# Sinkhorn-sorted attention feeding a gated MLP: the last batch's spatial products in two token parts, output tiles in load buffers, and a new hand-written order

## The chip, the cores and the metric

The kernel runs on one core of a Trainium2 chip. A core has five engines that run their own instruction streams and wait for each other by semaphores: TensorE (PE; its weight loads are shown as PEld), VectorE (DVE), ScalarE (ACT), GpSimd (POOL) and SyncE (SP). Sixteen DMA engines move data between HBM and the on-chip memory; here POOL issues the loads, which also cast f32 to bf16, and SP issues copies on the chip, transposes and the stores. The metric is the device time of one execution in microseconds; the time before is 164.44 us, the median of 3 runs (163.99 to 164.55).

## The reference

Two modules in a row, for 4 batches, 768 tokens, 8 heads of 64. The sequence is cut into 8 blocks of 96 tokens. A Sinkhorn-normalised 8x8 matrix for each batch and head mixes the blocks of K and V, attention runs inside each block, and a gated MLP with a spatial (token by token) product follows.

```python
P = sort_net
for _ in range(5):
    P = P - np.max(P, axis=-1, keepdims=True)
    P = np.exp(P)
    P = P / (np.sum(P, axis=-1, keepdims=True) + 1e-09)
    P = P / (np.sum(P, axis=-2, keepdims=True) + 1e-09)
k_sorted = np.einsum('bhij,bhjcd->bhicd', P, k_b)      # blocks of k mixed
v_sorted = np.einsum('bhij,bhjcd->bhicd', P, v_b)
scores = scale * np.matmul(q_b, k_sb.transpose(0, 1, 2, 4, 3))
attn = softmax(scores)
x = concat_heads(np.matmul(attn, v_sb))                # (4, 768, 512)
h = np.maximum(x @ w_in, 0.0)                          # d_ff = 1024
u, v = h[..., :512], h[..., 512:]
v_n = (v - mean(v)) / np.sqrt(var(v) + 1e-06)
v_s = np.einsum('ts,bsd->btd', w_spatial, v_n) + b_spatial[None, :, None]
out = (u * v_s) @ w_out
```

## The kernel before

The whole program is a list of short units, written out by hand in the string `ORDER` (from line 18) and issued in that order; no scheduler moves anything. Each engine gets its own part of every unit, in the order of the list, so a unit's place sets its place in each engine's queue. PSUM is four tiles, ps0 to ps3; most units name the tile that they use, and a unit must wait until the tile's last reader is done. A letter A, D or P in a unit names the engine that copies its result or multiplies: ACT, DVE or POOL.

The units, with the lines of their main instructions in the profile:

- `S0`, `SK` (L231 to L244): the Sinkhorn rounds, on ACT and DVE alone. `MC` (L210) and `MA` (L204) spread the identity and make a mask; `MB` (L207) casts the mask. `DM` (L219): matmuls on zeros that keep PE busy at the start.
- `PR` (L249) replicates the normalised matrices with PE; `P0` (L263, DVE) and `PC` then `PD` (L275, POOL) make the mixing matrices `pd`.
- `L` issues a load on POOL. Load tiles come from one pool of 8 buffers, `ld`. Loads are numbered onto 8 semaphore lanes, so a load's issue also waits for the landing of the load eight before it.
- `QT`, `QQ` (L307): q transposed. `KT` (L363): K mixed and transposed in one matmul, then copied to one of `NK` = 5 tiles `kt`; with two letters (AD, DA) the copy is made in two halves, one on each engine. `VT`, `VB` (L363, L381): the same for V of batch 0; `VM` (L390) and `VC` (L403, eight copies by SP for a batch) for V of the others.
- `SC` (L422, then the exponential on ACT, L427): scores of two heads and four blocks. `AT` (L468; L475 and L476 on DVE): attention times V, divided by the sums. `XT` (L498) or, for batches 2 and 3, `XD` (L486, a DMA transpose): the result turned for the MLP.
- `VP` (L514; relu on L113 ACT or L115 DVE): the v half of x @ w_in. `ST`, `LN`, `LA` (L531, L537, L543): its statistics and normalisation. `UP` (L557): the u half. `WT` (L504): the spatial weights turned.
- `SP` (L569): one spatial product, 128 features by all 768 tokens, 12 matmuls of 384 columns; DVE adds the bias (L575) into a tile `z` (two buffers). `GT` (L585): u times z into `gt`, on DVE or POOL. `BI` (L188) loads the bias.
- `OP` (L595): the output product for two tiles of 128 tokens, 16 matmuls of 512 columns (or fewer, when it is given a range of the four feature chunks); `OE` (L107 ACT or L109 DVE) copies it out of PSUM into a tile `o_sb`, two buffers; `OS` (L610) stores it.
- `CK` (L618 to L622), `CF` (L634 to L636), `LF` (L639): checks that the sums of the fast path stay in range, reduces them to a flag, and loads the flag into a register on every engine. At the end of the program a branch on that register goes to a general path, which is not taken here.

Where the order stands around the change: the last stage begins with `VP` of batch 3; its four `SP`, `GT` and the output products end the list, with `CK` and the last `OP` parts mixed, and `CF:2 LF` as the last two units.

Of the kernel before, what the change touches and what calls it, by code (L numbers as in the profile page):

```python
# [23 lines left out]
AT:0:0:1:1 SC:2:0:1:0 SC:3:0:2:1 AT:1:0:3:1 VM:2:A:1:0 AT:0:0:1:0 VM:3:A:1:1 AT:1:0:2:1 VM:2:A:1:2 XT:0:D:0:1:0
KT:3:A:1:2 AT:1:0:2:0 KT:0:A:1:0 AT:2:0:3:0 XT:3:A:0:1:2 KT:0:A:1:3 QQ:1:D:1:0 VM:2:A:1:3 XT:0:D:0:0:2 XT:3:D:0:0:0
SC:1:1:0:0 QQ:2:D:1:2 VC:1:0:4 KT:0:A:1:1 VP:1:D:0:0:1 SC:3:1:2:1 ST:0:0 SC:0:1:3:1 VP:2:A:0:4:5 WT:3:A:5 WT:1:D:4
VP:0:A:0:3 ST:0:5 PD:2:0:4 SC:2:1:1:0 ST:0:3 SC:1:1:2:0 UP:3:A:0:1:0 VP:2:A:0:2 VC:1:4:8 ST:0:1 ST:0:4 AT:0:1:0:0
ST:0:2 WT:1:A:3 SC:3:1:3:0 LN:0:0:6 UP:2:A:0:0:1 AT:0:1:2:0 AT:1:1:3:0 LA:0:0 PD:2:4:8 UP:3:A:0:1:1 WT:0:D:0 LA:0:2
# [5 lines left out]
OE:A:0:2 L:k:3:0:8 AT:1:2:3:1 VM:2:A:3:2 UP:3:A:1:1:0 ST:1:5 AT:0:2:2:1 ST:1:3 VM:2:D:3:1 L:q:3:0:8 UP:1:A:1:0:1
AT:3:2:1:1 LN:1:0:6 UP:0:A:1:1:1 LA:1:1 AT:1:2:3:0 OP:2:0:0 LA:1:0 SC:1:2:0:1 SC:0:2:2:0 OP:3:0:4 LA:1:5 OS:0:2
OE:D:0:0 LA:1:3 LA:1:4 LA:1:2 AT:2:2:0:1 AT:0:2:2:0 SP:1:1:0 OE:A:0:4 XD:2:1 SC:2:2:0:0 KT:0:DA:3:2 QQ:3:D:3:2
KT:1:D:3:1 KT:2:AD:3:0 SP:0:1:2 KT:2:A:3:3 OS:0:4 GT:D:1:0 QQ:1:A:3:0 AT:3:2:1:0 AT:0:2:0:0 VP:2:D:2:4:5 VC:3:0:4
VC:3:4:8 SC:3:3:3:0 SC:1:3:3:1 ST:2:4 XD:2:0 SP:0:1:1 SC:2:3:2:1 GT:D:1:2 SC:1:3:1:1 SP:3:1:3 AT:0:3:3:0 GT:P:1:3
AT:2:3:3:1 VP:1:A:2:2:3 ST:2:5 VP:0:A:2:0:1 OS:0:0 AT:1:3:2:1 GT:P:1:1 ST:2:3 UP:2:D:2:0:1 OP:1:1:2 SC:3:3:0:0
OE:D:1:2 ST:2:2 SC:2:3:1:0 UP:0:A:2:1:0 SC:1:3:0:1 ST:2:1 ST:2:0 LN:2:0:6 SC:3:3:2:0 UP:2:D:2:0:0 AT:0:3:1:1 LA:2:5  # L40
LA:2:4 LA:2:2 OS:1:2 UP:1:A:2:1:1 OP:2:1:0 AT:1:3:0:0 OE:A:1:0 LA:2:0 LA:2:3 LA:2:1 OP:3:1:4 AT:2:3:1:0 AT:0:3:2:0
SP:1:2:1 XD:3:0 AT:2:3:0:1 XD:3:1 GT:D:2:1 OE:A:1:4 SP:0:2:0 SP:1:2:3 GT:D:2:0 SP:0:2:2 OS:1:4 UP:3:D:3:0:0 OS:1:0
VP:0:D:3:2:3 GT:D:2:2 VP:1:A:3:0:1 ST:3:3 GT:D:2:3 ST:3:2 UP:3:A:3:0:1 VP:0:A:3:4:5 ST:3:1 OP:3:2:2 ST:3:0 OP:2:2:0
# [19 lines left out]
def kernel(  # L63
# [538 lines left out]
    def u_OE(eng, b, n0, lo=0, hi=2):  # L602
        b, n0, lo, hi = int(b), int(n0), int(lo), int(hi)
        if ("o", b, n0) not in st:
            st["o", b, n0] = moe.tile([128, 2, DM], FP32, name="o_sb", tag="o", bufs=2)
        copy(eng, st["o", b, n0][:, lo:hi], st["o_ps", b, n0][:, lo:hi])

    def u_OS(b, n0, lo=0, hi=2):
# [4 lines left out]
        )  # L613

    def u_CK():
        nc.vector.memset(bad, 0.0)  # L618
# [109 lines left out]
```

## Time and profile before

| | us |
|---|---|
| median of 3 runs | 164.44 |
| the profiled execution, its own time | 163.99 |
| its span in the profile | 162.2 |
| PE busy | 147.9 (91%) |
| DVE busy | 117.7 (73%) |
| ACT busy | 84.3 (52%) |
| POOL busy | 33.7 (21%) |

| line | engine, operation | count | mean ns |
|---|---|---|---|
| L569 | PE, spatial product, 384 columns | 192 | 326 |
| L595 | PE, output product, 512 columns | 93 shown of 96 | 379 |
| L575 | DVE, z = product + bias, 768 columns | 16 | 957 |
| L585 | DVE, u times z, 768 columns | 9 | 948 |
| L585 | POOL, u times z, 768 columns | 7 | 1640 |
| L107 / L109 | ACT / DVE, copy of 1024 output columns | 7 / 2 | 1012 / 1219 |
| L107 / L109 | ACT / DVE, copy of 512 output columns | 5 / 1 | 588 / 692 |
| L107 / L109 | ACT / DVE, whole K copy, 768 columns | 7 / 2 | 800 / 952 |
| L107 / L109 | ACT / DVE, half K copy, 384 columns | 7 / 7 | 482 / 549 |
| L476 | DVE, attention result divided | 32 | 687 |
| L543 | DVE, normalisation of 512 columns | 24 | 402 |

Mean times of matmuls contain the depth of the pipeline; in a run of many, a matmul of 512 columns follows the one before after about 0.213 us. A busy PE is therefore not PE at its peak, and the idle time before an instruction says what it waited for.

### The profile page before, as it was taken

How to read it: one execution, taken by the hardware profiler on the slowest of the kernel's cores; microseconds unless marked ns; L12 is line 12 of the kernel's file. 1: busy time of each engine (PE TensorE's matmuls, PEld its weight loads, DVE VectorE, ACT ScalarE, POOL GpSimd, SP SyncE). 2: the span in 40 equal slices, each digit the busy share in tenths (PEclk: the TensorE clock that was granted, in tenths of full speed). 3: DMA queues.
4: the chain of work that ended last, by engine and by line, in shares of the span. 5: the costliest groups of instructions: out<-in, count | busy, mean ns of one | idle time of the engine just before them, and what ended most of it. 6: DMA issues, size and time to landing. Idle time of an engine off the chain costs nothing.

```text
span 162.2 us, 3967 instructions
## 1 busy us (share of the span) xinstructions
PE 147.9 (91%) x1646; PEld 89.5 (55%) x1657; DVE 117.7 (73%) x265; ACT 84.3 (52%) x118; POOL 33.7 (21%) x39
## 2 busy tenths in 40 slices
...
GB/s 12 191 204 205 203 205 205 210 220 237 271 206 204 206 172 0 69 133 148 184 188 94 225 149 195 0 36 97 0 107 237 113 0 0 91 172 129 129 250 25
DMA packets 27351, 23.20 MB, mean 143 GB/s; under 512 B 7232, under 2 KB 24128, under 8 KB 27328
## 3 DMA queue, kind: packets, MB, share of 16 engines
...
q14 instruction: 9, 0.07, 0.1%
HBM read 24.78 MB, written 6.29 MB: 192 GB/s over the span
## 4 chain that ended last, share of the span: by engine, by line
PE 78%; ACT 7%; DVE 6%; DMA 2%; issue 2%; DVEq 0%; ACTq 0%
PE ps L569 20%; PE ps L557 13%; PE ps L514 13%; PE ps L595 11%; PE ps L468 4%; PE ps L422 4%; PE ps L363 3%; PE ps L390 3%; PE ps L307 3%; ACT ex L427 2%; ACT kt L107 2%; PE ps L498 2%; DMA out_dram<-o_sb 1%; PE ps L504 1%; ACT o_sb L107 1%
## 5 line engine op out<-in xcount | busy, mean ns | idle before, releaser
L569 PE MATMUL ps<-wspT,v_sb 128*128 128x384 bf16 x192 | 33.2, 326 | 0.0
L427 ACT ACTIVATE ex<-ps 96x768 bf16<-96x768 f32 x32 | 24.4, 806 | 12.4 <-PE ps L422 12.3
L585 POOL TENSOR_TENSOR gt<-z,u_sb 128x768 bf16<-128x768 f32 x7 | 11.4, 1640 | 92.7 <-DVE z L575 42.1
L569 PEld LDWEIGHTS <-v_sb 128*128 128x128 bf16 x192 | 18.2, 98 | 11.9 <-issue 0.2
L575 DVE TENSOR_TENSOR z<-ps,b_bc 128x768 f32<-128x768 f32 x16 | 15.3, 957 | 11.6 <-PE ps L569 11.5
L557 PE MATMUL ps<-xT,w_in_sb 128*128 128x384 bf16 x128 | 23.3, 326 | 0.0
L476 DVE TENSOR_TENSOR x_sb<-ps,rec_all 96x512 bf16<-96x512 f32 x32 | 22.0, 687 | 1.1
L514 PE MATMUL ps<-w_in_sb,xT 128*128 128x512 bf16 x89 | 22.2, 379 | 0.4
L595 PE MATMUL ps<-w_out_sb,gt 128*128 128x512 bf16 x93 | 22.0, 379 | 0.2
L107 ACT COPY o_sb<-ps 128x1024 f32<-128x1024 f32 (+1 forms) x12 | 9.8, 835 | 14.8 <-PE ps L595 12.9
L531 DVE BATCH_NORM_STATS2 stats<-v_sb 128x6 f32<-128x512 bf16 x24 | 16.2, 677 | 1.0 <-ACT v_sb L113 0.9
L113 ACT ACTIVATE v_sb<-ps 128x1024 bf16<-128x1024 f32 (+1 forms) x8 | 7.4, 920 | 17.6 <-PE ps L514 17.6
L557 PEld LDWEIGHTS <-w_in_sb 128*128 128x128 bf16 x128 | 11.8, 98 | 7.6
L595 PEld LDWEIGHTS <-gt 128*128 128x128 bf16 x96 | 9.2, 98 | 10.2
L514 PEld LDWEIGHTS <-xT 128*128 128x128 bf16 x96 | 9.0, 98 | 9.6 <-DVE x_sb L476 0.2
L113 ACT ACTIVATE u_sb<-ps 128x768 bf16<-128x768 f32 x13 | 10.6, 812 | 5.1 <-PE ps L557 5.0
L107 ACT CAST kt<-ps 128x768 bf16<-128x768 f32 (+1 forms) x14 | 8.7, 641 | 7.9 <-PE ps L363 5.5
L468 PEld LDWEIGHTS <-ex 96*128 96x128 bf16 x256 | 10.5, 97 | 3.6 <-issue 0.3
L468 PE MATMUL ps<-vb,ex 96*128 96x65 bf16 x256 | 11.9, 193 | 0.1
L219 PE MATMUL ps<-warm 128*128 128x512 bf16 x35 | 9.9, 436 | 1.3 <-DVE warm L192 1.3
L422 PE MATMUL ps<-qT,kt 64*128 64x96 bf16 x256 | 9.5, 204 | 1.6 <-ACT kt L107 1.3
L422 PEld LDWEIGHTS <-kt 64*128 64x128 bf16 x256 | 6.2, 94 | 6.9 <-issue 3.8
...
## 6 DMA issues: line engine op xcount, KB each, us to landing
...
```

Source lines behind the costliest of these rows:

```text
L107: nc.scalar.copy(out=out, in_=in_)
L113: nc.scalar.activation(out=out, in_=in_, func=AF.Relu)
L422: nc.tensor.matmul(t[:, hh, 0:HW].rearrange("p (g x) -> p g x", g=G)[:, :, ii * TB:(ii + 1) * TB], lhsT=kT[rows, i * BLK:i * BLK + 128], r ...
L427: nc.scalar.activation(out=e_tile(b, hp, ih).rearrange("p h (x g) -> p h x g", g=G), in_=t[0:BLK, :, 0:HW].rearrange("p h (g x) -> p h x g ...
L468: nc.tensor.matmul(t[:, hh, ii * VW:ii * VW + D + 1], lhsT=e[:, c:c + 128], rhs=vb[b % 2][:, ih * NI + ii, 2 * hp + hh, 0:D + 1], start=Tr ...
L476: nc.vector.tensor_mul(out=x_sb[:, hp].rearrange("p i (h d) -> p h i d", h=2), in0=tv[:, :, :, 0:D], in1=_raw_ap(rec, 0, [rec.ap[0], [NI, ...
L514: nc.tensor.matmul(t[:, x, :], lhsT=st["xT", b][:, n // 3, kc, (n % 3) * 128:(n % 3 + 1) * 128], rhs=w_in_sb[:, kc, DH:DFF], start=(kc == ...
L531: nc.vector.bn_stats(out=stats, in_=st["v_sb", b, n])
L557: nc.tensor.matmul(t[:, x, 0:HW], lhsT=w_in_sb[:, kc, mc * 128:(mc + 1) * 128], rhs=st["xT", b][:, ih, kc, :], start=(kc == 0), stop=(kc = ...
L569: nc.tensor.matmul(t[:, x, 0:HW], lhsT=st["v_sb", b, n][:, mc * 128:(mc + 1) * 128], rhs=wspT[:, 3 * x:3 * x + 3, n, :], start=(n == 0), s ...
L575: nc.vector.tensor_add(out=z.rearrange("p (x c) -> p x c", x=2), in0=t[:, :, 0:HW], in1=b_bc.rearrange("p (x c) -> p x c", x=2),)
L595: nc.tensor.matmul(t[:, x, :], lhsT=st["gt", b, mc][:, (n0 + x) * 128:(n0 + x + 1) * 128], rhs=w_out_sb[:, mc, :], start=(mc == 0), stop=( ...
```

## The change

The helpers gain two sizes, and the output tiles move to the load pool:

```diff
-    NE = 5
+    NE, NK, NZ, NX = 5, 6, 3, 4
...
-    NK = 5
...
-            st["x", b, ih] = att.tile([BLK, HP, NI, 128], BF16, name="x_sb", tag="x", bufs=3)
+            st["x", b, ih] = att.tile([BLK, HP, NI, 128], BF16, name="x_sb", tag="x", bufs=NX)
...
-        z = moe.tile([128, S], FP32, name="z", tag="z", bufs=2)
+        z = moe.tile([128, S], FP32, name="z", tag="z", bufs=NZ)
...
-            st["o", b, n0] = moe.tile([128, 2, DM], FP32, name="o_sb", tag="o", bufs=2)
+            st["o", b, n0] = ld.tile([128, 3, DM], FP32, name="o_sb", tag="ld")[:, 0:2]
```

New units for the last batch: `SH` is a spatial product for tokens 0 to 511 (part 0) or 512 to 767 (part 1), with its own bias sum; `GH` multiplies one part by u; `OH`, `OI` and `OJ` make, copy and store the output of one token tile for a range of columns. (Two more new units, `WW` and `XX`, are not in the order.)

```diff
+    def u_SH(ps, b, mc, c):
+        t, x = ps_tile(ps)[:, 0], tokens(c)
+        w = x.stop - x.start
+        for n in range(G):
+            nc.tensor.matmul(
+                t[:, 0:w], lhsT=st["v_sb", b, n][:, mc * 128:(mc + 1) * 128],
+                rhs=wspT[:, x.start // 128:x.stop // 128, n, :],
+                start=(n == 0), stop=(n == G - 1),
+            )
+        st["z", b, mc, c] = z = moe.tile([128, S], FP32, name="z", tag="z", bufs=NZ)[:, 0:w]
+        nc.vector.tensor_add(out=z, in0=t[:, 0:w], in1=b_bc[:, x])
+    def u_GH(eng, b, mc, c):
...
+        eng.tensor_mul(out=st["gt", b, mc][:, x], in0=st["z", b, mc, c], in1=st["u", b, mc // 2][:, mc % 2, x])
+    def u_OH(ps, b, n, c0, c1, lo=0, hi=4):
...
+        for mc in range(lo, hi):
+            nc.tensor.matmul(
+                st["o1_ps", b, n, c0], lhsT=st["gt", b, mc][:, n * 128:(n + 1) * 128], rhs=w_out_sb[:, mc, c0:c1],
...
+    def u_OI(eng, b, n, c0, c1):
+        st["o1", b, n, c0] = ld.tile([128, 3, DM], FP32, name="o1_sb", tag="ld")[:, 0, 0:c1 - c0]
+        copy(eng, st["o1", b, n, c0], st["o1_ps", b, n, c0])
+    def u_OJ(b, n, c0, c1):
+        nc.sync.dma_start(out=out[b, n * 128:(n + 1) * 128, c0:c1], in_=st["o1", b, n, c0])
```

The order is written anew from end to end. Its beginning, the part where batch 2's K begins, and its end:

```diff
-S0 CO SK:0 L:q:0:0:8 L:k:0:0:8 L:v:0:0:8 L:v:1:0:8 BH SK:1 SK:2 L:k:1:0:8 ID IV:2 MC IV:0 DM:1:6:512 L:q:1:0:8 SK:3
-L:wv MA DM:3:6:512 DM:1:6:512 DM:2:6:512 SK:4 L:wsb QT:1:A:0:0 MB QT:0:D:0:1 QT:3:A:0:2 DM:2:6:512 PR:3 DM:2:6:512
-P0:0:2 KT:1:A:0:0 P0:6:8 L:wu P0:4:6 PC:D P0:2:4 PD:1:0:4 QT:0:D:0:3 L:wsa IV:1 PD:1:4:8 KT:2:DA:0:1 KT:3:DA:0:3
+S0 CO L:q:0:0:8 SK:0 L:k:0:0:8 ID SK:1 DM:1:6:512 DM:2:6:512 SK:2 MC L:v:0:0:8 DM:0:6:512 MA L:v:1:0:8 IV:0 L:k:1:0:8
+SK:3 L:q:1:0:8 DM:1:6:512 DM:3:6:512 DM:2:6:512 SK:4 QT:1:A:0:0 PR:2 MB QT:0:A:0:3 P0:6:8 P0:4:6 L:wv L:wu L:wsa
+P0:2:4 P0:0:2 QT:3:D:0:1 PC:A KT:1:A:0:1 KT:0:A:0:0 BH PD:1:4:8 L:wsb QT:3:D:0:2 IV:2 KT:2:D:0:2 SC:1:0:1:1 L:v:2:0:8
+SC:0:0:0:0 PD:1:0:4 KT:3:D:0:3 SC:2:0:1:0 L:k:2:0:8 VT:1:D:0:1 SC:0:0:2:0 SC:3:0:0:1 VT:2:D:0:0 VB:0:D:0:1 VT:1:A:0:2
...
-GT:P:0:3 KT:1:AD:2:3 KT:3:AD:2:2 KT:0:DA:2:0 KT:2:A:2:1 GT:P:0:2 QQ:1:A:2:0 SC:0:2:3:0 VM:3:D:2:3 SP:2:0:1 VM:1:A:2:2
+SP:1:0:1 SP:2:0:2 SC:0:1:2:0 AT:1:1:0:0 KT:3:A:2:3 GT:P:0:2 XT:2:A:1:1:2 KT:0:D:2:1 KT:3:A:2:0 QQ:1:D:2:0 GT:P:0:1
+QQ:2:D:2:2 KT:0:A:2:2 AT:3:1:2:0 SP:1:0:0 SC:3:2:0:0 XT:0:D:1:1:0 XT:2:A:1:0:0 XT:1:D:1:0:2 AT:3:2:0:0 SC:0:2:1:0
...
-SP:3:3:0 GT:P:3:2 SP:0:3:1 OP:2:2:4 GT:D:3:1 OS:2:0 OS:2:2 OE:A:2:4 GT:D:3:0 SP:3:3:3 OP:1:3:0:0:3 GT:D:3:3
-OP:0:3:4:0:3 OP:-1:3:0:3:4 OE:A:3:0:1:2 OP:3:3:2:0:3 CK OS:2:4 OP:-1:3:2:3:4 OE:D:3:2:1:2 OE:A:3:0:0:1 OP:-1:3:4:3:4
-OS:3:0:1:2 OS:3:0:0:1 OE:A:3:2:0:1 OS:3:2:0:1 OS:3:2:1:2 OE:A:3:4:0:1 OS:3:4:0:1 OE:A:3:4:1:2 OS:3:4:1:2 CF:2 LF
+CK OE:D:1:0 SP:3:2:3 GT:P:2:3 CF:0 SP:2:2:2 VP:0:A:3:0:1 VP:1:D:3:2:3 VP:3:A:3:4:5 ST:3:2 ST:3:5 OS:0:4 SP:2:2:0
+ST:3:1 SP:3:2:1 GT:P:2:0 UP:0:A:3:0:1 GT:D:2:2 ST:3:3 UP:2:A:3:0:0 UP:3:A:3:1:0 ST:3:4 ST:3:0 LN:3:0:6 LF LA:3:0
+GT:P:2:1 OP:2:2:0 OS:1:2 OE:D:2:0 LA:3:2 OP:0:2:4 LA:3:3 LA:3:5 OP:3:2:2 OE:A:2:2 LA:3:4 LA:3:1 OS:1:0:0:1 OS:1:0:1:2
+SH:2:3:0:0 GH:P:3:0:0 OS:2:2:0:1 OS:2:2:1:2 SH:1:3:1:0 OS:1:4 OE:A:2:4 GH:D:3:1:0 SH:0:3:2:0 UP:1:D:3:1:1 GH:D:3:2:0
+OS:2:0:0:1 OS:2:0:1:2 SH:2:3:3:0 SH:3:3:0:1 SH:1:3:1:1 GH:P:3:3:0 OS:0:0 GH:D:3:0:1 OS:2:4:0:1 OS:2:4:1:2 SH:0:3:3:1
+SH:2:3:2:1 OP:3:3:0 GH:P:3:1:1 OE:D:3:0 GH:P:3:2:1 OP:2:3:2 GH:P:3:3:1 OH:3:3:5:0:256:0:4 OI:D:3:5:0:256 OE:A:3:2
+OS:3:0 OH:1:3:4:0:512:0:4 OJ:3:5:0:256 OI:D:3:4:0:512 OS:3:2 OH:2:3:5:256:512:0:4 OI:A:3:5:256:512 OJ:3:4:0:512
+OJ:3:5:256:512
```

In it every K copy is whole (11 on ACT, 5 on DVE); of the products u times z, 10 whole ones and 5 parts are POOL's, 2 whole ones and 3 parts DVE's; `CK`, `CF` and `LF` stand before or within the last batch's MLP; and `BI` stands between the two `VC` of batch 1.

More of the change, by code (lines that the diff above doesn't have):

```diff
@@ L24 @@
[L24 to L28, printed above, removed]
@@ L34 @@
[L34 to L38, printed above, removed]
@@ L39 @@
[L39 to L43, printed above, removed]
@@ L44 @@
-ST:3:5 ST:3:4 OE:A:2:2 LN:3:0:6 UP:1:A:3:1:1 LA:3:1 UP:0:A:3:1:0 LA:3:5 LA:3:3 LA:3:0 LA:3:2 OE:A:2:0 LA:3:4 SP:1:3:2
-SP:3:3:0 GT:P:3:2 SP:0:3:1 OP:2:2:4 GT:D:3:1 OS:2:0 OS:2:2 OE:A:2:4 GT:D:3:0 SP:3:3:3 OP:1:3:0:0:3 GT:D:3:3
-OP:0:3:4:0:3 OP:-1:3:0:3:4 OE:A:3:0:1:2 OP:3:3:2:0:3 CK OS:2:4 OP:-1:3:2:3:4 OE:D:3:2:1:2 OE:A:3:0:0:1 OP:-1:3:4:3:4
-OS:3:0:1:2 OS:3:0:0:1 OE:A:3:2:0:1 OS:3:2:0:1 OS:3:2:1:2 OE:A:3:4:0:1 OS:3:4:0:1 OE:A:3:4:1:2 OS:3:4:1:2 CF:2 LF
+S0 CO L:q:0:0:8 SK:0 L:k:0:0:8 ID SK:1 DM:1:6:512 DM:2:6:512 SK:2 MC L:v:0:0:8 DM:0:6:512 MA L:v:1:0:8 IV:0 L:k:1:0:8
@@ new lines @@
+SK:3 L:q:1:0:8 DM:1:6:512 DM:3:6:512 DM:2:6:512 SK:4 QT:1:A:0:0 PR:2 MB QT:0:A:0:3 P0:6:8 P0:4:6 L:wv L:wu L:wsa
+P0:2:4 P0:0:2 QT:3:D:0:1 PC:A KT:1:A:0:1 KT:0:A:0:0 BH PD:1:4:8 L:wsb QT:3:D:0:2 IV:2 KT:2:D:0:2 SC:1:0:1:1 L:v:2:0:8
+SC:0:0:0:0 PD:1:0:4 KT:3:D:0:3 SC:2:0:1:0 L:k:2:0:8 VT:1:D:0:1 SC:0:0:2:0 SC:3:0:0:1 VT:2:D:0:0 VB:0:D:0:1 VT:1:A:0:2
+VB:3:D:0:0 VT:0:A:0:3 L:q:2:0:8 AT:2:0:1:1 L:wo VB:1:A:0:2 PD:2:0:4 AT:3:0:1:0 VM:0:D:1:1 VM:2:A:1:2 VM:1:A:1:0
+VM:3:A:1:3 AT:2:0:0:0 IV:1 VB:0:D:0:3 L:v:3:0:8 SC:1:0:3:0 VC:1:4:8 AT:2:0:2:0 SC:3:0:2:1 AT:0:0:3:0 BI SC:1:0:3:1
@@ new lines @@
+KT:2:A:1:3 AT:3:0:0:1 XT:1:A:0:0:2 AT:0:0:3:1 XT:2:A:0:0:0 XT:3:D:0:1:0 VC:1:0:4 KT:1:A:1:1 QQ:0:D:1:2 KT:2:A:1:0
+PD:2:4:8 KT:3:A:1:2 QQ:1:A:1:0 AT:0:0:2:1 VP:2:D:0:0:1 SC:3:1:3:1 XT:0:D:0:1:2 VP:1:D:0:2 SC:3:1:0:1 ST:0:2 ST:0:0
+SC:2:1:1:0 VP:0:A:0:4:5 VP:1:A:0:3 ST:0:1 ST:0:5 ST:0:3 SC:3:1:1:1 ST:0:4 SC:2:1:2:1 UP:0:A:0:1:0 UP:3:A:0:0:1
+AT:1:1:1:1 L:k:3:0:8 AT:2:1:3:1 LN:0:0:6 PD:3:4:8 L:q:3:0:8 PD:3:0:4 UP:0:A:0:1:1 LA:0:1 AT:1:1:0:1 LA:0:0
+UP:3:A:0:0:0 LA:0:5 WT:2:A:0 LA:0:2 WT:0:D:5 LA:0:3 WT:1:A:1 WT:3:D:4 WT:0:D:2 SC:2:1:3:0 AT:3:1:2:1 VM:1:A:2:1
@@ new lines @@
+WT:0:D:3 LA:0:4 VM:2:A:2:3 SC:3:1:0:0 VM:1:A:2:0 VM:0:D:2:2 VC:2:4:8 SP:2:0:3 AT:3:1:1:0 VC:2:0:4 AT:0:1:3:0 GT:D:0:3
+SP:1:0:1 SP:2:0:2 SC:0:1:2:0 AT:1:1:0:0 KT:3:A:2:3 GT:P:0:2 XT:2:A:1:1:2 KT:0:D:2:1 KT:3:A:2:0 QQ:1:D:2:0 GT:P:0:1
+QQ:2:D:2:2 KT:0:A:2:2 AT:3:1:2:0 SP:1:0:0 SC:3:2:0:0 XT:0:D:1:1:0 XT:2:A:1:0:0 XT:1:D:1:0:2 AT:3:2:0:0 SC:0:2:1:0
+VM:2:A:3:2 VP:1:A:1:2:3 GT:P:0:0 VM:0:A:3:3 AT:2:2:1:0 ST:1:3 VP:3:D:1:4:5 VM:0:A:3:0 VM:2:D:3:1 VP:1:A:1:0:1
+SC:0:2:3:0 SC:2:2:0:1 ST:1:5 OP:3:0:2 ST:1:0 ST:1:4 OE:A:0:2 VC:3:4:8 ST:1:2 SC:0:2:3:1 SC:1:2:1:1 UP:2:A:1:1:0
@@ new lines @@
+UP:3:A:1:0:1 VC:3:0:4 ST:1:1 AT:1:2:3:0 UP:0:D:1:0:0 LN:1:0:6 LA:1:3 LA:1:1 SC:3:2:2:1 SC:1:2:2:0 OP:2:0:0 KT:1:D:3:1
+OE:A:0:0 KT:3:A:3:2 QQ:0:A:3:2 OS:0:2 LA:1:2 AT:2:2:2:0 LA:1:5 LA:1:0 LA:1:4 AT:1:2:3:1 OP:3:0:4 XD:2:0 AT:0:2:0:1
+OE:A:0:4 UP:2:A:1:1:1 AT:3:2:1:1 AT:1:2:2:1 XD:2:1 SP:0:1:0 SC:1:3:2:0 QQ:2:D:3:0 KT:3:D:3:3 GT:P:1:0 KT:0:A:3:0
+VP:1:D:2:0:1 SC:2:3:0:1 SC:3:3:1:0 VP:0:A:2:4:5 AT:3:3:2:0 AT:1:3:0:1 ST:2:4 SP:2:1:2 ST:2:1 ST:2:0 GT:P:1:2
+SC:3:3:0:0 SC:1:3:3:1 VP:0:A:2:2:3 AT:2:3:1:0 ST:2:2 SP:1:1:3 SC:2:3:3:0 ST:2:5 GT:P:1:3 SC:0:3:2:1 SP:3:1:1 ST:2:3
@@ new lines @@
+SC:0:3:1:1 AT:2:3:0:0 UP:1:A:2:1:1 AT:0:3:3:0 LN:2:0:6 GT:P:1:1 UP:3:A:2:0:1 UP:1:A:2:1:0 LA:2:1 AT:2:3:3:1 AT:0:3:1:1
+OP:3:1:2 AT:2:3:2:1 LA:2:3 OE:A:1:2 LA:2:2 UP:0:A:2:0:0 OP:2:1:0 LA:2:5 LA:2:0 OP:0:1:4 XD:3:0 XD:3:1 LA:2:4 OE:A:1:4
+CK OE:D:1:0 SP:3:2:3 GT:P:2:3 CF:0 SP:2:2:2 VP:0:A:3:0:1 VP:1:D:3:2:3 VP:3:A:3:4:5 ST:3:2 ST:3:5 OS:0:4 SP:2:2:0
+ST:3:1 SP:3:2:1 GT:P:2:0 UP:0:A:3:0:1 GT:D:2:2 ST:3:3 UP:2:A:3:0:0 UP:3:A:3:1:0 ST:3:4 ST:3:0 LN:3:0:6 LF LA:3:0
+GT:P:2:1 OP:2:2:0 OS:1:2 OE:D:2:0 LA:3:2 OP:0:2:4 LA:3:3 LA:3:5 OP:3:2:2 OE:A:2:2 LA:3:4 LA:3:1 OS:1:0:0:1 OS:1:0:1:2
@@ L448, in u_SM @@
         nc.vector.reduce_max(out=top, in_=tv, axis=AX.X)
-        low = moe.tile([128, S], FP32, name="low", tag="z", bufs=2)[0:BLK].rearrange("p (h i c) -> p h i c", h=2, i=NI)
+        low = moe.tile([128, S], FP32, name="low", tag="z", bufs=NZ)[0:BLK].rearrange("p (h i c) -> p h i c", h=2, i=NI)
         nc.vector.tensor_sub(out=low, in0=tv, in1=_raw_ap(top, 0, [top.ap[0], [NI, 2], [1, NI], [0, BLK]]))
```

37 lines of the change are left out of this document (31 added, 6 removed).

## The prediction

> **What bounds the kernel now.** I read the chain of waits first, then a table of stretches, then the timeline at the two places where the table shows PE idle. The chain by engine:
>
> ```profile
> PE 78%; ACT 7%; DVE 6%; DMA 2%; issue 2%; DVEq 0%; ACTq 0%
> ```
>
> 78% of 162.2 us is 126.5 us of matmuls. The stretches (start:end, length, busy time and count of PE, weight loads, DVE, ACT, POOL, then granted clock, DMA share, GB/s):
>
> ```profile
> 0.00:11.84 11.84, 9.91 (x74) 4.53 (x76) 8.14 (x48) 3.93 (x8) 8.69 (x17) 1.00 0.92 134
> 32.80:50.00 17.20, 17.09 (x224) 11.12 (x223) 13.73 (x32) 14.11 (x21) 3.04 (x3) 1.00 1.23 232
> 50.00:60.00 10.00, 9.13 (x155) 6.66 (x154) 7.05 (x14) 5.33 (x9) 3.28 (x2) 1.00 1.28 203
> 100.00:120.00 20.00, 19.89 (x180) 11.27 (x179) 16.95 (x37) 9.10 (x12) 3.24 (x2) 1.00 0.12 39
> 120.00:135.00 15.00, 14.95 (x81) 7.83 (x80) 13.04 (x21) 3.84 (x4) 0.00 (x0) 1.00 0.51 115
> 147.60:153.00 5.40, 5.40 (x27) 2.31 (x24) 3.86 (x14) 1.07 (x2) 0.00 (x0) 1.00 0.38 145
> 153.00:162.20 9.20, 0.07 (x1) 0.00 (x0) 0.53 (x3) 1.66 (x3) 0.00 (x0) 0.79 0.43 150
> ```
>
> From 32.8 to 153 PE is idle only around 57 us, at full clock. So a new order can win only in the first 33 us (Sinkhorn, then short links PE, copy, PE), at that spot, and in the 9.2 us behind the last matmul (147.63 + 5.34 = 152.97). The spot:
>
> ```profile
> 57.18 1.49 DVE L109 CAST kt<-ps 128x384 bf16<-128x384 f32 x3 [0.60 <-ACT kt L107]
> 57.79 0.86 PE L307 MATMUL ps<-ident,q_in 128*64 128x128 bf16 x24 [0.29 <-DVE kt L109]
> 58.70 1.18 ACT L107 CAST kt<-ps 128x384 bf16<-128x384 f32 x2 [1.17 <-DVE kt L109]
> 59.23 0.34 PE L422 MATMUL ps<-qT,kt 64*128 64x96 bf16 x8 [0.58 <-ACT kt L107]
> ```
>
> The two halves of one K copy run one after the other, and PE waits for them. The end, from the chain in order of time (start, us, what):
>
> ```profile
> 151.34 0.60 ACT o_sb L107
> 151.95 2.21 DMA out_dram<-o_sb
> ...
> 154.32 1.07 ACT o_sb L107 x2
> ```
>
> The last output copies stand behind a store, because its tile is to be used again. They end at 155.40; the last store is issued at 155.79, the span ends 6.4 us after that.
>
> **The change, part by part.** All sums are against the profiled execution, 163.99 us (span 162.2 and 1.8 around it); the median of the runs is 164.44, 0.45 more.
>
> *Work.* PE keeps its columns: four spatial products of 12x384 become 24x512 + 24x256. The last output product has 28 matmuls instead of 24 for the same columns; with the fill of a few more groups +0.1 us (0 to 0.3). VectorE gives up products: 9 at 0.948 become 2, plus parts of 512, 512 and 256 columns, by its copies (1024 columns 1.22, 512 0.69, so 256 about 0.43) 1.38 + 0.43; that is 8.5 to 3.7 us. Other moves give some back (one transposed-q and one v_mix copy more at 0.96, copies of the output +1.7). POOL takes 10 whole products at 1.64 and five parts.
>
> *Head.* m32 (0.37) now stands with spread (0.41) in one gap of the Sinkhorn chain; each had a gap of its own under ACT's exponential. The next row sum starts about 0.37 later (0 to 0.4). All 36 warm-up matmuls come ahead of the first transpose: 24 end at 8.29, 12 more at 0.213 end near 10.9, before p_t at 11.4; the six that lay between the replication (to 11.84) and the first K product (13.17) are gone. But that K product needs heads 2 and 3, now third of four P0 at 0.41, so it starts near 13.5. ACT takes prep_sb behind VectorE's four P0 (same PSUM tile), then two K copies at 0.80, so the first score exponential begins at about 16.0; before, 15.97. Stepping on, PE, copy, PE, I reach the first v product at 32.4 to 32.8 with a transpose (0.34) and a score (0.28) less done; before, 32.85. Head: 0 us (-0.6 to +1.0).
>
> *Loads.* POOL issues wv seventh as before; wu, then wsa, wsb and v of batch 2 come before q and k of batch 2. At 205 GB/s 768 KB take 3.84 us, 512 KB 2.56, 576 KB 2.88. From q at 8.8 (1.26 + its least 7.5): wv 30.6, v of batch 2 about 42.7. The vb copies of batch 1 and the bias leave SP some 6 us earlier (31.3 to about 25.5; bias between them), 1.2 MB, so up to 5.9 us of queue: wv by 36.5, v by 48.6. Issue to first byte cost 3 to 4 us there, so wv is nearly through: 0 (0 to +2.5). PE reaches the first v mix of batch 2 14.7 us of work after 32.8, at 47.5: 0 (0 to +1.1). Behind the load of wo POOL holds the pd of batch 2, wanted only from 48 us on: nothing.
>
> *Transition.* From 55.3 to 59.6 PE does XT 0.34, four K at 0.335, q 0.67, a score 0.28: 2.6 us of work, so 1.7 is wait. A whole copy is 0.80 (ACT) or 0.95 (DVE) against 0.55 + 0.48 in turn, and the sixth kt buffer lets K go ahead. The bound is -1.7; but VectorE has by then 1 to 2 us more work behind it than before at the same PE work (each unit's count by its row), with z, x and q copies queued in front; taken -0.8 (-1.7 to +0.5). From 60 to 95 PE loses about one more us against its rows (VectorE 86% busy from 72 to 85); with fewer products there -0.3 (-1 to +0.5).
>
> *Early flag.* Every engine now reads the flag in mid-stream:
>
> ```profile
> L639 DVEq TENSOR_LOAD <-flag x1: 543/543/543, 153.6 to 153.6; - x1
> L639 PEldq TENSOR_LOAD <-flag x1: 490/490/490, 153.6 to 153.6; - x1
> L639 SPq TENSOR_LOAD <-flag x1: 912/912/912, 156.2 to 156.2; - x1
> ```
>
> On PE the output products of batch 2 queue behind it: +0.4 (0 to 0.5). On DVE it lies in the 0.6 us wait for rstd. At the end it saves nothing: SP read it while the last stores were in flight.
>
> *Last stage, PE side.* The first part-product of the last batch needs all six normalised v tiles; VectorE has them about 0.3 before PE gets there. Then POOL's product of the last quarter, 512 columns, 1.1 us by 1.64 x 512/768, ends about when the output product wants it: +0.3 (0 to 1.2).
>
> *Tail.* With T the last matmul's end: ACT's 1024-column copy (1.01) starts at T-1.7 and is done before the last 256 columns, whose copy (about 0.4) ends near T+0.5; VectorE's 512 columns end at T+0.5 too. No store is waited for, since load buffers are free. Two issues of 0.35: the last starts at T+0.85, against T+2.8: -2.0. Behind it the backlog is alike (896 KB in 1.5 us against 1 MB in 1.8) and the last piece is 128 KB: -0.2 more (-0.8 to +0.3 beside a bound of -1.6 for the issue).
>
> Sum: 0.1 + 0 + 0 - 0.8 - 0.3 + 0.4 + 0.3 - 2.2 = -2.5, so 161.5 as profiled, 161.95 by the median; I say **161.8**.
>
> One rule speaks against so many products on POOL. No POOL product of this trace overlaps a VectorE product; beside one (141.36 to 143.0) VectorE's z sum took 0.958, its usual time, but it has only one input in SBUF. The Trainium skill ("SBUF — State Buffer", section "SBUF: two separate sides") says that the two engines share a port pair as an exclusive lock: a VectorE operation with two SBUF inputs and a GpSimd operation that reads SBUF block each other for the whole instruction. No run here shows it yet; it is rival C.
>
> **The rivals.**
> *A, slower: VectorE becomes the bound between 33 and 71 us.* By units and rows that stretch holds 26 us of VectorE work before (26.35 measured in 36.1 us) and 31.5 after, for 33 of PE. It was never over 87% busy for long (13.04 of 15). At 87% the stretch takes 36.2, no loss; at 80% 39.4, 3.3 more, and the 0.8 gain there is gone: 161.8 + 4.1 = 165.9. It decides from some 83% down. For: z, x and q copies free the PSUM buffers that PE needs next. Against: PE's own waits made half of VectorE's idle time.
> *B, the change hides nothing but the tail's issue order:* the stores' backlog ends when it did, since the same 1.5 MB leaves last; tail -0.8 for -2.2 and no transition gain: 161.8 + 1.4 + 0.8 = 164.0, no change. Against: the last copy and issue really move.
> *C, products on VectorE and POOL exclude each other:* the 256-column product of the last batch waits up to 1.1 us for POOL's, once or twice, and normalisations up to 1.6: +1.2, 163.0.
> *D, a late load* (wv or v of batch 2): +2 us, 163.8.
>
> **How the numbers follow.** Forecast 52%, A 20%, B 9%, C 11%, D 8%. About 0.3% (0.5 us) is what a measurement can tell from no change. Faster is the forecast, C, most of D and a light A: 0.72; same 0.08; slower, the rest of A and stacked stalls, 0.20. The forecast's own range is 160.2 to 163.2; with A and the rest 160.0 to 165.4.
>
> **What would show it.** Tail: last matmul to span end near 7 us; no output copy waiting for a store. Transition: no K copies of 384 columns, PE's wait there under 1 us. Flag: a 0.5 us read on PE before the output products of batch 2. Head: first v product within 1 us of 32.8. Wrong, if PE's busy share falls between 33 and 71 us with DVE as releaser (A), or if POOL and VectorE products stretch where they overlap (C).

## The result, and the profile after

The changed kernel takes 162.07 us (median of 4 runs, 161.73 to 162.65) against 164.26 for the kernel before beside it (4 runs, 163.99 to 164.55): ratio 0.987, 95% interval 0.9835 to 0.9905. It is faster by 1.3%, the way that was forecast; 161.8 was said. The profiled execution took 162.01; its span is 160.1. T stands below for the end of the last matmul of the output.

The chain of waits by engine:

```profile
PE 76%; DVE 8%; ACT 6%; DMA 4%; issue 1%
```

The stretches, with the columns of the prediction's table:

```profile
32.80:50.00 17.20, 17.14 (x196) 10.51 (x194) 14.26 (x33) 12.73 (x20) 5.25 (x6) 1.00 1.22 232
50.00:60.00 10.00, 10.00 (x154) 7.03 (x154) 8.16 (x13) 4.40 (x6) 2.27 (x2) 1.00 1.26 225
60.00:72.00 12.00, 12.00 (x142) 7.10 (x138) 9.23 (x16) 6.39 (x9) 2.62 (x2) 1.00 1.15 185
...
120.00:135.00 15.00, 15.00 (x84) 8.02 (x82) 9.93 (x18) 4.87 (x7) 5.16 (x3) 1.00 0.19 71
...
153.00:160.10 7.10, 0.00 (x0) 0.00 (x0) 0.33 (x1) 0.37 (x1) 0.00 (x0) 0.66 0.47 159
```

PE is now busy without a gap from 50 to 72 us. Yet T is 152.98, as before, and the 2.1 us between the spans lie behind it: 7.11 us follow T, against 9.22. That the two agree to the hundredth is chance: in seven profiled executions of the new order with whole K copies T lies between 152.67 and 153.69, in three of the old order with the old tail and split copies between 152.85 and 153.19. So a few tenths of T in one pair of executions show nothing by themselves. The end, from the timeline (start, length, what; in brackets the idle time before it and its releaser):

```profile
152.64 0.69 DVE L111 COPY o_sb<-ps 128x512 f32<-128x512 f32 x1 [0.49 <-PE ps L666]
153.02 0.37 ACT L109 COPY o_sb<-ps 128x256 f32<-128x256 f32 x1 [0.72 <-PE ps L666]
153.52 2.21 SPq L678 DMA_DIRECT2D out_dram<-o_sb  x2
```

No copy waits for a store; the last ends 0.41 behind T (2.42 before), and the last store is issued at 153.97 (155.79 before). The spot near 57 us:

```profile
57.71 0.80 ACT L109 CAST kt<-ps 128x768 bf16<-128x768 f32 x1
...
58.06 1.02 PE L364 MATMUL ps<-pd,k_in 128*64 128x128 bf16 x24
...
58.63 0.96 DVE L111 CAST kt<-ps 128x768 bf16<-128x768 f32 x1 [0.22 <-PE ps L364]
58.89 1.53 PE L308 MATMUL ps<-ident,q_in 128*64 128x128 bf16 x48
```

K copies are whole, and no PE line has a bracket. So why does PE not end earlier? The PE groups by line from the start to the first v product, before (0 to 32.84):

```profile
L422 PE MATMUL ps<-qT,kt 64*128 64x96 bf16 x72 | 3.1, 205 | 1.1 <-ACT kt L107 0.7 <-DVE vb L109 0.2 <-ACT ex L427 0.2
...
L498 PE MATMUL ps<-ident,x_sb 96*128 96x96 bf16 x32 | 1.9, 206 | 0.0
```

and after (0 to 32.48):

```profile
L423 PE MATMUL ps<-qT,kt 64*128 64x96 bf16 x64 | 2.7, 205 | 0.3 <-ACT kt L109 0.3
...
L499 PE MATMUL ps<-ident,x_sb 96*128 96x96 bf16 x24 | 1.4, 206 | 0.0
```

In this pair the first v product starts 0.36 earlier, but one score (8 matmuls) and one transpose (8) are still to do: 0.62 us by the prediction's prices. That is a loss of 0.26 by equal work. From the first v product to T it takes 120.50 us, against 120.14: without the 0.62, 0.26 less. The two cancel.

One pair is little, and the runs below repeat both parts. Kernels that are the same up to the first v product start it at 32.54, 32.54 and 32.84 in the old order and at 32.32 to 33.19 (six executions) in the new: on average at 32.64 and 32.66, so the 0.36 is not confirmed. From there to T, kernels that differ in the flag, the hint or the output buffers alone take 120.14, 120.31 and 120.64 in the old order and 120.30, 120.32, 120.50 and 120.50 in the new. By these means the head loses some 0.6 by equal work and the stretch behind it gains some 0.6. The sizes are uncertain by a few tenths; that they cancel stands.

### The profile page after: what moved, and what is told of

The parts are those of the page before. It is cut to its first block, busy times and chain, and to the rows that moved or that the text cites. A ratio compares the mean times of both kernels' runs of the same rounds, so it can differ in the third digit from the quotient of the medians.

```text
span 160.1 us, 3999 instructions
## 1 busy us (share of the span) xinstructions
PE 149.1 (93%) x1661; PEld 89.6 (56%) x1661; DVE 115.5 (72%) x265; ACT 81.3 (51%) x111; POOL 44.1 (28%) x47
## 4 chain that ended last, share of the span: by engine, by line
PE 76%; DVE 8%; ACT 6%; DMA 4%; issue 1%
PE ps L590 14%; PE ps L578 13%; PE ps L535 12%; PE ps L616 12%; PE ps L646 5%; PE ps L469 4%; PE ps L423 3%; PE ps L364 3%; DMA xT<-x_sb 3%; PE ps L391 2%; PE ps L499 2%; ACT kt L109 2%; PE ps L308 2%; ACT ex L428 2%; DVE x_sb L477 2%; PE ps L505 1%
## 5 line engine op out<-in xcount | busy, mean ns | idle before, releaser
L606 POOL TENSOR_TENSOR gt<-z,u_sb 128x768 bf16<-128x768 f32 x10 | 17.0, 1706 | 76.1 <-ACT ex L428 42.2
L590 PE MATMUL ps<-wspT,v_sb 128*128 128x384 bf16 x144 | 25.1, 326 | 0.0
L578 PE MATMUL ps<-xT,w_in_sb 128*128 128x384 bf16 x128 | 22.6, 326 | 0.0
L616 PE MATMUL ps<-w_out_sb,gt 128*128 128x512 bf16 x88 | 20.2, 379 | 0.0
L109 ACT COPY o_sb<-ps 128x1024 f32<-128x1024 f32 (+1 forms) x9 | 8.4, 943 | 20.5 <-PE ps L616 19.8
L590 PEld LDWEIGHTS <-v_sb 128*128 128x128 bf16 x144 | 13.6, 98 | 8.7
L115 ACT ACTIVATE u_sb<-ps 128x768 bf16<-128x768 f32 x14 | 11.4, 814 | 9.6 <-PE ps L578 9.5
L596 DVE TENSOR_TENSOR z<-ps,b_bc 128x768 f32<-128x768 f32 x12 | 11.5, 955 | 5.5 <-PE ps L590 4.0
L616 PEld LDWEIGHTS <-gt 128*128 128x128 bf16 x88 | 8.3, 98 | 9.2
L476 DVE RECIPROCAL rec_all<-ps 96x8 f32<-96x8 f32 x32 | 6.3, 196 | 8.6 <-PE ps L469 8.4
```

The costliest lines, as they stand in the source:

```text
L109: nc.scalar.copy(out=out, in_=in_)
L115: nc.scalar.activation(out=out, in_=in_, func=AF.Relu)
L578: nc.tensor.matmul(t[:, x, 0:HW], lhsT=w_in_sb[:, kc, mc * 128:(mc + 1) * 128], rhs=st["xT", b][:, ih, kc, :], start=(kc == 0), stop=(kc = ...
L590: nc.tensor.matmul(t[:, x, 0:HW], lhsT=st["v_sb", b, n][:, mc * 128:(mc + 1) * 128], rhs=wspT[:, 3 * x:3 * x + 3, n, :], start=(n == 0), s ...
L606: eng.tensor_mul(out=gt, in0=st["z", b, mc], in1=st["u", b, mc // 2][:, mc % 2])
L616: nc.tensor.matmul(t[:, x, :], lhsT=st["gt", b, mc][:, (n0 + x) * 128:(n0 + x + 1) * 128], rhs=w_out_sb[:, mc, :], start=(mc == 0), stop=( ...
```

## The experiments

Each kernel ran beside the kernel before (medians 164.06 to 164.13). T and the span behind it are from one profiled execution each.

| run | median us | ratio, 95% interval | T | span behind T |
|---|---|---|---|---|
| old_order_new_tail | 162.17 | 0.9892 (0.9875 to 0.9909) | 153.06 | 7.32 |
| new_order_old_tail | 162.94 | 0.9935 (0.9922 to 0.9948) | 152.82 | 8.01 |
| old_load_buffers | 164.21 | 1.0 (0.9991 to 1.0008) | 153.19 | 9.37 |
| flag_late | 161.67 | 0.9865 (0.9838 to 0.9891) | 152.75 | 6.97 |
| flag_late_hint | 160.87 | 0.9798 (0.9781 to 0.9815) | 152.92 | 5.81 |
| early_hint | 162.14 | 0.9877 (0.9861 to 0.9893) | 153.69 | 7.15 |
| old_whole_k | 163.27 | 0.9942 (0.9927 to 0.9958) | 152.40 | 9.57 |
| products_apart | 162.23 | 0.9884 (0.9868 to 0.9899) | 153.41 | 7.05 |
| old_best | 160.16 | 0.9753 (0.9737 to 0.977) | 151.98 | 6.53 |
| new_ma_hint | 160.68 | 0.9796 (0.9778 to 0.9814) | 152.67 | 5.78 |
| old_hint | 163.99 | 0.9992 (0.998 to 1.0003) | 152.85 | 9.30 |
| new_split_k | 164.10 | 1.0003 (0.9987 to 1.0019) | 155.19 | 7.03 |

### Which half of the change holds the gain

old_order_new_tail is the order of before with the changed last stage and the flag behind the normalisation of batch 3 (K copies split as before; the numbers of buffers are those of the change); new_order_old_tail is the changed kernel, its early flag included, with the old last stage.

```diff
-SP:1:3:2 SP:3:3:0 GT:P:3:2 SP:0:3:1 OP:2:2:4 GT:D:3:1 OS:2:0 OS:2:2 OE:A:2:4 GT:D:3:0 SP:3:3:3 OP:1:3:0:0:3 GT:D:3:3
+CK SH:1:3:0:0 GH:P:3:0:0 SH:3:3:1:0 CF:2 GH:D:3:1:0 SH:0:3:2:0 OP:2:2:4 GH:D:3:2:0 OS:2:0 OS:2:2 SH:1:3:3:0 OE:A:2:4
...
```

> The order of before up to the last batch's spatial products, then the token parts, part outputs and load buffers of the change. Theory (the whole gain lies behind the last matmul, 9.23 us to 7.12 us, and the rest of the new order is worth nothing): 2.0 us under before, ratio 0.986 to 0.990, last matmul near 153, span end 7.1 after it. Rival (the new order carries part of the gain, the tail only moves a wait): less than 1 us under before.

> The new order up to the last batch's spatial products, then four whole spatial products and the output by feature chunks as in before, but with output tiles in load buffers. Theory: the last matmul stays near 153 and about 8.5 to 9 us follow it (only the 0.4 us wait for a store is gone), so 0 to 0.6 us under before. Rival (the order before the tail is what gained): 1.5 us or more under before.

The new tail in the old order gives the whole gain (0.9892 against 0.987, their intervals overlap). The new order with the old tail was expected to give 0.6 us at most and gives 1.2, a miss: the gain lies behind T (8.01 against 9.22), where the early flag and the load buffers are new. The buffers give nothing (next experiment). The trace's single records point to the flag: with the branch decided early, the last 16 KB packet of program code came at 150.96, ahead of the last four stores, and the last store's bytes landed 2.6 us after its issue. Before, that packet came at 156.01, while those stores were moving, and it took 3.6. No run has the old order with an early flag alone. The gains of the two halves, 2.0 and 1.2, do not add up to the change's 2.2.

### Load buffers alone

```diff
-            st["o", b, n0] = moe.tile([128, 2, DM], FP32, name="o_sb", tag="o", bufs=2)
+            st["o", b, n0] = ld.tile([128, 3, DM], FP32, name="o_sb", tag="ld")[:, 0:2]
```

> The kernel before with its output tiles taken from the load buffers, nothing else. Theory: the last two copies no longer wait for a store (0.37 us of idle on ACT), so the last store is issued 0.3 to 0.5 us earlier and the time falls by 0.2 to 0.5 us; the other 1.6 us of the tail come from the parts. Rival: the store's landing at 154.2 was what set the end and 1 us or more goes.

The last copies in its timeline, no longer released by a store:

```profile
153.52 1.56 ACT L107 COPY o_sb<-ps 128x512 f32<-128x512 f32 x3 [1.38 <-DVE o_sb L109]
```

They end 1.89 behind T instead of 2.42, and nothing is gained, where 0.2 to 0.5 was expected. The last store's issue still comes 2.75 behind T (2.81 before): the first of the last four stores goes out after the copy that ACT makes behind VectorE's (154.13), the others 0.45, 0.46 and 0.90 behind one another, as before (0.46, 0.50, 0.86). What the last gap holds, the trace does not show; it is not the copy, which ended 0.86 ahead of the issue. The wait that the chain of waits names lay beside the issues, not ahead of them.

### The flag and the end of the program

flag_late is the changed kernel with `CF` and `LF` at the very end again. The hint is the program's note to an engine of where the branch at the end probably goes; before and after give it to PE and VectorE, and flag_late_hint, early_hint and old_hint give it to ACT too.

```diff
-CK OE:D:1:0 SP:3:2:3 GT:P:2:3 CF:0 SP:2:2:2
+CK OE:D:1:0 SP:3:2:3 GT:P:2:3 SP:2:2:2
...
-LN:3:0:6 LF LA:3:0
+LN:3:0:6 LA:3:0
...
-OJ:3:5:256:512
+OJ:3:5:256:512 CF:0 LF
...
-            "general", hint="LikelyTaken", engines=[mybir.EngineType.PE, mybir.EngineType.DVE])
+            "general", hint="LikelyTaken", engines=[mybir.EngineType.PE, mybir.EngineType.DVE, mybir.EngineType.Activation])
```

> The changed kernel with only the flag's matmul and the loads of the flag put back at the end of the list. Theory (the loads in mid-stream cost nothing, since PE's sequencer made its 487 ns load while the array was busy, and at the end SP's load runs while the last stores are in flight): within 0.3 us of the changed kernel. Rival of the prediction (0.4 us of PE time given back): 0.4 us faster than the changed kernel. Rival for the early flag (the end was held by it): 0.5 to 1 us slower than the changed kernel.

> The changed kernel with the flag at the end of the list, and with the branch hint given to ACT too (it had PE and VectorE alone). Theory: with the late flag the stores had all landed 3.7 us before the span's end, and the end waited for ACT, whose first event behind its branch came 4.3 us after it; with the hint that falls to under 1 us, the end is set by the stores (landed at 156.0) and 0.6 to 1.1 us go: 160.6 to 161.1. Rival (ACT's 4.3 us is no fetch of the code behind the branch, or the hint does nothing on ACT): within 0.3 us of the kernel with the late flag alone, 161.7.

> The changed kernel as it is (early flag) with the branch hint given to ACT too. Theory (there the end is set by the last store, whose bytes share the DMA engines with code fetches that begin at 153.7, not by ACT, which was done 1.2 us before): within 0.3 us of the changed kernel, 161.8 to 162.3. Rival (ACT's fetch is among what holds the stores): 0.4 us or more faster.

> Before with nothing changed but the branch hint given to ACT too. In before ACT's first record behind the branch is at 158.85 and the last store's bytes land at 159.35, so ACT's slow branch is covered by the stores: no change, ratio 0.998 to 1.002. Rival: the code fetch itself delays the stores, and taking ACT's out of the way gains 0.3 or more.

First the flag's place in mid-stream. The changed kernel's flag reads (duration in ns, start in us):

```profile
L702 SPq TENSOR_LOAD <-flag x1: 474/474/474, 119.7 to 119.7; - x1
...
L702 PEldq TENSOR_LOAD <-flag x1: 487/487/487, 130.7 to 130.7; - x1
L702 DVEq TENSOR_LOAD <-flag x1: 546/546/546, 133.8 to 133.8; - x1
```

PE's sequencer reads at 130.7, while the array is busy with the u products until 133.5: the output products behind it do not wait, and PE was busy all of the 15 us from 120 to 135. So the 0.4 us that the prediction charged was 0. The median of flag_late alone would not tell: it is 0.40 below the changed kernel's, as the rival has it that was named before the run, but the intervals overlap.

But the early flag costs something at the end. The stores issued from 152 us on (size, us from issue to landing), in the changed kernel:

```profile
out_dram<-o_sb SPq DMA_DIRECT2D x1, 512.0 KB, 4.8
out_dram<-o_sb SPq DMA_DIRECT2D x2, 128.0 KB, 3.1
out_dram<-o_sb SPq DMA_DIRECT2D x1, 256.0 KB, 4.6
```

and in flag_late, the same stores:

```profile
out_dram<-o_sb SPq DMA_DIRECT2D x1, 512.0 KB, 2.9
out_dram<-o_sb SPq DMA_DIRECT2D x2, 128.0 KB, 2.6
out_dram<-o_sb SPq DMA_DIRECT2D x1, 256.0 KB, 2.7
```

With the flag known early, engines come to the branch some 1.5 us sooner (ACT at 153.03, in flag_late at 154.48), before the last stores have gone. Two queues of kind "instruction", which the page counts among what the 16 DMA engines moved, bring program code in packets of 16 KB and 8 KB. In the trace's single records:

| | 16 KB code packet at the end: start, took | last store: issue took, bytes landed | ACT: branch, its next event | span |
|---|---|---|---|---|
| after | 153.69, 1.66 us | 1.76 us, 158.00 | 153.03, 157.26 | 160.1 |
| flag_late | 155.92, 1.34 | 0.61, 155.99 | 154.48, 158.76 | 159.7 |
| flag_late_hint | 156.16, 1.37 | 0.63, 156.17 | 154.67, 155.15 | 158.7 |

In the changed kernel the packet falls among the last stores, the last issue takes 1.76 us (the one before it 0.34), and its bytes land 2 us later than in flag_late. With the flag late the stores are through 2 us earlier, and still 0.4 us at most is gained (161.67 against 162.07, the intervals overlap), because something else ends last. SP's waits of flag_late at the end (waiting line, what it waited for; us, times, longest):

```profile
SPq L786 <- ACTq L759: 1.1, 1, 1.1
```

L759 is ACT's branch. ACT's event after it comes 4.3 us later; PE and VectorE, which have the hint, need 0.45 and 0.60 us. (POOL and SP need 0.2 without it, so not every engine without the hint is slow.) With the hint ACT needs 0.48, the line is gone, and 0.8 us are gained: 0.9798, an interval below those of flag_late and of the changed kernel. Neither helps where another end is last: the hint with an early flag changes nothing (162.14, the last issue 1.80 us again), nor does it in the kernel before (0.9992), whose bytes land at 159.35, behind ACT's event at 158.85. The three runs with the hint came as expected. That the packet itself stretches the stores, and not another thing about the early branch, is read from their times; no run moved the packet alone. It is not ACT's code: with the hint for ACT it comes all the same (early_hint: at 154.38, for 1.71 us). The Trainium skill ("Runtime: NRT & Kernel Launch", section "Instruction fetch mechanics") says that code comes in blocks of 16 KiB over a DMA queue of the sequencer's own, and that a taken branch to a target outside the two blocks at hand waits for the fetch. The packets of 16,384 bytes agree, those of 8,192 on the second queue do not; ACT's 4.3 us would fit such a wait, but the trace does not say which packet ends it.

### Whole K copies

old_whole_k makes the seven split K copies of before whole, new_split_k splits seven of the changed kernel's.

```diff
-KT:1:AD:2:3 KT:3:AD:2:2 KT:0:DA:2:0
+KT:1:A:2:3 KT:3:A:2:2 KT:0:D:2:0
...
```

> The kernel before with its seven split K copies made whole, on the engine named first; nothing else. Theory (half copies run one after the other, 0.55 + 0.48 us, against 0.80 or 0.95 whole, and PE waited for them at 57 and 16 us): PE's wait near 57 us shrinks by 0.3 to 0.6 us, 0.1 to 0.6 us under before. Rival (two engines together free the PSUM sooner; the wait is the queue, not the copy): no faster or slower.

> The changed kernel with seven of its whole K copies split over two engines again, as before had them. In the old order whole copies gained 0.8. If they are worth as much in the new one, this is 0.6 to 1.0 slower than the changed kernel: 162.8, the last matmul ending near 153.8. Rival: the sixth kt buffer and the new order already take K off PE's path near 57 us, and the split costs 0 to 0.3: 162.2.

In old_whole_k the spot near 57 us has no PE wait either, with five kt buffers and the order of before:

```profile
57.04 2.21 ACT L108 CAST kt<-ps 128x768 bf16<-128x768 f32 x3
57.58 0.96 DVE L110 CAST kt<-ps 128x768 bf16<-128x768 f32 x1 [0.62 <-PE ps L364]
57.89 0.86 PE L308 MATMUL ps<-ident,q_in 128*64 128x128 bf16 x24
```

T falls by 0.58, below all three of the kernels with split copies, the median by 0.8, a little over the 0.1 to 0.6 expected. In the new order the split costs 2.0 us (164.10 against 162.07; T 2.2 later), twice the most that either theory said. Where, in new_split_k's timeline and stretches:

```profile
83.29 0.48 ACT L109 CAST kt<-ps 128x384 bf16<-128x384 f32 x1 [1.55 <-DVE kt L111]
...
84.57 0.82 ACT L109 CAST kt<-ps 128x768 bf16<-128x768 f32 x1
84.73 0.64 PE L469 MATMUL ps<-vb,ex 96*128 96x65 bf16 x16 [1.07 <-ACT o_sb L109]
```

```profile
72.00:85.00 13.00, 11.71 (x156) 6.95 (x157) 7.99 (x18) 9.85 (x15) 0.00 (x0) 1.00 0.51 104
```

ACT waits 1.55 us for VectorE's half, its output copy behind that is late, and PE loses 1.3 us from 72 to 85, where the changed kernel loses none; where the rest of the 2.2 goes was not followed. So seven whole copies (not all of the same heads) are worth 2 us in the new order and 0.8 in the old one; the rest of the new order gives back what they bring.

### Products on VectorE and POOL

products_apart gives two of VectorE's products (one whole, one part of 256) to POOL:

```diff
-SP:2:2:2 VP:0:A:3:0:1
+SP:2:2:2 GT:P:2:2 VP:0:A:3:0:1
...
-GT:P:2:0 UP:0:A:3:0:1 GT:D:2:2 ST:3:3
+GT:P:2:0 UP:0:A:3:0:1 ST:3:3
...
-GH:D:3:0:1
+GH:P:3:0:1
```

> The changed kernel with two VectorE products (feature chunk 2 of batch 2, part 1 of chunk 0 of batch 3) given to POOL, so that no product of VectorE runs beside one of POOL. Theory (the two exclude each other, which stretched POOL's product at 130.76 from 1.64 to 2.29 us, and two parts near 147 by 0.5 and 0.2 us, but PE covers it): POOL's products all at 1.64, 1.15 and 0.67 us, time within 0.3 us of the changed kernel. Rival (the lock costs the path time): 0.4 us or more faster. Rival (the stretch has another cause): the stretched products stay.

In the changed kernel's timeline products overlap twice:

```profile
130.59 0.95 DVE L606 TENSOR_TENSOR gt<-z,u_sb 128x768 bf16<-128x768 f32 x1
130.76 2.29 POOL L606 TENSOR_TENSOR gt<-z,u_sb 128x768 bf16<-128x768 f32 x1 [0.24 <-DVE z L596]
...
146.34 1.97 POOL L659 TENSOR_TENSOR gt<-z,u_sb 128x512 bf16<-128x512 f32 x2 [4.26 <-DVE z L652]
146.86 0.92 DVE L659 TENSOR_TENSOR gt<-z,u_sb 128x256 bf16<-128x256 f32 x1
```

POOL's whole product takes 2.29 us instead of 1.64; VectorE's 256 columns take 0.92 instead of the prediction's 0.43 (an estimate; VectorE's products of 768 and 512 columns, 0.947 and 0.692, give 0.44). POOL's groups in products_apart (busy, mean ns; then idle) have their plain durations:

```profile
L607 POOL TENSOR_TENSOR gt<-z,u_sb 128x768 bf16<-128x768 f32 x11 | 18.0, 1641 | 75.0 <-ACT ex L429 42.8 <-DVE z L597 19.9 <-DVE ends L699 12.4
L660 POOL TENSOR_TENSOR gt<-z,u_sb 128x256 bf16<-128x256 f32 x4 | 2.6, 670 | 0.0
```

The time stays (162.23): the 0.65 and 0.5 us lie under PE's work. The prediction cites an exclusive lock for this from the Trainium skill ("SBUF — State Buffer", section "SBUF: two separate sides"). The trace agrees in the main: who comes second loses most of what the other had left, 0.65 of 0.78 us and 0.49 of 0.64, where a full block would take all of it. VectorE operations with one input in PSUM were not stretched (z sums of 768 columns 0.957 throughout).

### The parts put together

old_best is old_whole_k's order with the new tail and buffers, the late flag and the hint; new_ma_hint is flag_late_hint with `MA` moved back to a Sinkhorn gap of its own.

```diff
-SK:2 MC L:v:0:0:8 DM:0:6:512 MA L:v:1:0:8 IV:0 L:k:1:0:8 SK:3 L:q:1:0:8
+SK:2 MC L:v:0:0:8 DM:0:6:512 L:v:1:0:8 IV:0 L:k:1:0:8 SK:3 MA L:q:1:0:8
```

> The order of before with its seven two-engine K copies made whole, the last stage of the changed kernel (token parts, output tiles in load buffers), the flag made and read at the very end, and the branch hint given to ACT too. If the parts add up (K copies 0.8, tail about 2.0, end of program 1.2 off about 164.1): 160.0 (159.6 to 160.5), the last matmul ending near 152.4 and the span 5.8 behind it. Rival: the gain of whole K copies is taken back by the last stage's waits for VectorE and POOL, which all come after it: 160.9, no better than the new order with the same end.

> The changed kernel with the flag late and the hint for ACT (160.87), and m32 moved back to a Sinkhorn gap of its own, behind the fourth step's units. If m32 and spread in one gap held the Sinkhorn chain up as the prediction priced it (0.2 to 0.4), p_t and the first v product come 0.2 to 0.4 earlier and the kernel gains 0 to 0.3: 160.6. Rival: the links PE, copy, PE behind p_t wait for other copies anyway, and nothing is gained: 160.8 to 160.9.

old_best, at 160.16, beats both kernels, and flag_late_hint, with a like tail and end, by 0.7 us, their intervals apart: the parts nearly add up. So the new order, taken by itself, is slower than the old one with whole K copies. The 0.62 us of PE work that its head leaves for later, for a start that is no earlier on average, is one part of it; the runs do not divide the rest. new_ma_hint gains 0.2 at most (intervals overlap): not settled.

## Why the prediction was right, step by step

- *Sum.* Forecast −2.5 for the profiled execution, measured −1.98. The tail was −2.2 and measured −2.11; all else was −0.3 and measured 0.0 at T (0.13 us more lies outside the span). The place of the gain was the right one. That both sums came so close is in part luck, since terms in them cancel.
- *Tail.* Issue: "the last starts at T+0.85" was T+0.99, against T+2.81, a gain of 1.82 for the 2.0 foreseen. Backlog: "-0.2 more" went the other way, +0.47; from the last issue to the last byte it took 4.02 us, against 3.55 before. The missing 0.76 came from a place that the sum does not have: from the last byte to the end of the span it took 2.10 us, against 2.86. No run takes that end apart. The span ended 7.11 behind T ("near 7 us").
- *Early flag.* "On PE the output products of batch 2 queue behind it: +0.4" was mis-sized: 0, because PE's sequencer runs ahead of its array. "At the end it saves nothing" missed that it costs: program code came among the last stores. Late and with the hint for ACT the kernel gains 1.2.
- *Head.* 0 forecast; +0.26 by equal work in the one pair, some +0.6 by the means. The start was foreseen (32.48, in the 32.4 to 32.8 said), and the prediction named the transpose and score less done, but it did not charge their 0.62.
- *Transition and 60 to 95.* −0.8 and −0.3, not confirmed in size: PE's waits went, and by equal work the whole stretch to T gained 0.26 in the one pair and some 0.6 by the means. The bound of 1.7 was too large from the start: the prediction's own table has PE idle for 0.87 us of the ten from 50 to 60. Taking away the waits in the old order gave 0.58 at T.
- *Last stage.* +0.3 forecast, not settled. With whole K copies in the old order, the new last stage (old_best) takes 119.47 us from the first v product to T, the old one (old_whole_k) 119.58; with split copies the new one takes 120.71 (old_order_new_tail), the old one 120.14 to 120.64.
- *Rival A.* VectorE was busy 31.65 us of the 39.2 from 32.8 to 72 (81%), right by its sum of 31.5 and below its 83%, and PE was full. Its rule, that a stretch is lost below 87% of VectorE, fell: PE had other work in that time.
- *Rival B.* Its time, no change, fell. Half of its mechanism was right: no gain of the transition is left at T.
- *Rival C.* The mechanism is there, its price 0: PE had other work.
- *Rival D.* The loads were in time, wv at 31.37 for a first use at 32.48, v of batch 2 at 47.08 for 47.96. But the step that was to delay them did not happen. That the vb copies of batch 1 "leave SP some 6 us earlier" was wrong: the first was issued at 31.18, against 31.28 before. SP waited 6.4 us for POOL's fill of vb (`IV:1`), which stands behind the load of wo in the new order.
